# An attention and MLP kernel's generated order, built anew with another rule for the lock between VectorE and GpSimd

## The chip, the cores and the metric

The kernel runs on one core of one Trainium2 chip. The metric is the device time of one execution in microseconds, given as a median of three runs. Smaller is better. A profile is one further execution, read instruction by instruction. Engines are named as the profile names them: PE (TensorE matmuls), PEld (its weight loads), DVE (VectorE), ACT (ScalarE), POOL (GpSimd) and SP (SyncE, which issues the DMAs; SPq is its queue).

## What is computed

```python
# q, k, v: (4, 12, 448, 64) float32; w_in (768, 2048); w_out (2048, 768)
scores = scale * np.matmul(q, k.transpose(0, 1, 3, 2))
scores = np.where(mask, -1000000000.0, scores)          # causal
scores = scores - np.max(scores, axis=-1, keepdims=True)
attn = np.exp(scores)
attn = attn / (np.sum(attn, axis=-1, keepdims=True) + 1e-09)
x = np.matmul(attn, v)                                  # then (1792, 768)
h = x @ w_in
g = np.where(h >= 1, h, np.where(h <= -1, 0.0, (h + 1) ** 2 / 4))
return g @ w_out
```

## The kernel before

**Stages.** There are 24 pairs of heads (4 batches of 6). For a pair the kernel loads q and k into `st` tiles, transposes them on DVE (L713), multiplies scores on PE (L835 for the first five pairs, L845 and L865 for the others), masks and takes the row maximum on DVE (L884), takes the exponential on ACT (L888), adds a small number to the row sum `su` (L894 on POOL or L896 on DVE), inverts it (L899, DVE), scales the row tile `e` (L769 POOL, L771 ACT or L772 DVE), transposes it on PE (L785), copies it out of PSUM into `pt` (L816 ACT or L821 DVE) and multiplies with v on PE (L913). The result `x` feeds the first MLP product (L608): 16 blocks of 128 columns of w_in for each batch, 18 matmuls a block, and behind each block ACT `r` (L618), DVE `vv` (L621) and a product `r` on DVE (L627) or, as two instructions, on POOL (L624 and L625). There is a single `vv` buffer. `r` is stored to DRAM (`g_scratch`).

The second MLP stage loads `z` from `g_scratch`, forms sums and products of blocks of seven (a scheme with seven products in place of eight), and multiplies on PE (L1028) in seven token pairs. The first of these token pairs also needs w_out's 56 blocks, read back from DRAM as `w2`, `wn`, `st`, `sr`, `w` and `w3` tiles.

**Split into two parts.** Every matmul operand outside the first five pairs' scores is split in a rounded part (a copy: L462 ACT, L463 DVE, L464 POOL) and a residual (a subtraction: L471 DVE, L472 POOL). So each of q (`tt`), k (`ks`), `x`, w_in (`w<-wn`), w_out (`w<-w` and its like) and `hl` costs one copy and one subtraction. The line numbers L462 to L472 are those of the helpers that all of them share.

**What sets the order.** No loop issues these instructions. All of them are tasks of a planner (`Plan`), each with one or more alternatives: an engine, a cost, a function. `run` plays the tasks against a clock of its own, picks at each step the task that can start first and the engine for it, and emits it. Each engine then runs its instructions strictly in that order. `solve` does this some 100 times, disturbing the due times between the plays by the fixed random numbers in `STEPS` (`shake`), and the last play is the program. An alternative is marked as holding a lock (the planner calls it `port`) that DVE and POOL share; `PEN` is a penalty in microseconds on leaving the first alternative for one on another engine.

The planner's PSUM tiles matter below: the first MLP stage's last blocks and the second stage's products take turns on the same `s` banks, four of them, so a product waits until `vv` (L621) has read the block that was there.

Of the kernel before, what the change touches and what calls it, by code (L numbers as in the profile page):

```python
# [15 lines left out]
ALU = mybir.AluOpType  # L16
# [17 lines left out]
class Task:  # L34
    def __init__(self, alts, prio):
# [5 lines left out]
        self.lat = 1.6  # L41

# [5 lines left out]
class Plan:  # L48
# [98 lines left out]
    def solve(self):  # L147
# [4 lines left out]
        for ahead in (22.0,):  # L152
            for pen in (0.4,):
                self.AHEAD, self.PEN = ahead, {"DVE": pen, "ACT": 0.1}
# [29 lines left out]
    )  # L184

    def shake(self, seed):

        rng = random.Random(seed)
# [6 lines left out]
        kind = rng.randrange(3)  # L195
# [15 lines left out]
    def run(self, dry=False):  # L211
# [9 lines left out]
        while left:  # L221
# [21 lines left out]
            for prio, _, s, t in can:  # L243
                e0, c0, _, p0 = t.alts[0]
                c0 = 0.0 if e0 == "PE" else c0
                own = max(s, free.get(e0, 0.0) + queued.get(e0, 0.0), port if p0 else 0.0) + c0
                for a, (e, c, _, p) in enumerate(t.alts):
# [3 lines left out]
                    if a and st + c + queued.get(e, 0.0) + self.PEN.get(e, 0.0) >= own:  # L251
                        continue
                    chosen.setdefault(e, []).append(((st, prio), t, a, st, 0.0 if e == "PE" else c))
                queued[e0] = queued.get(e0, 0.0) + c0
            for e, cands in chosen.items():
                first = min(cands, key=lambda x: x[0])
                limit = first[3] + self.LOOK * first[4]
                key, t, a, st, _ = min((x for x in cands if x[3] <= limit and x[0][1] <= first[0][1]),
                                       key=lambda x: (x[0][1], x[0][0]))
                if best is None or key < best[0]:  # L260
                    best = (key, t, a, st)
# [845 lines left out]
```

## Time and profile before

| what | value |
|---|---|
| device time, median of 3 runs | 633.13 us (631.77 to 633.73) |
| the profiled execution's own time | 630.88 us |
| its span, first to last instruction | 629.1 us |
| busy PE, DVE, ACT, POOL | 607.3, 467.3, 340.9, 208.5 us |
| granted TensorE clock | 1.00 up to 600 us, 0.98 behind it |

The profiled execution is 2.25 us below the median of the three timed runs and 0.89 us below the fastest of them. A busy PE includes the time in which a matmul is still in its pipeline, so two matmuls that follow each other overlap in that sum. "Idle" and "wait" rows count only the time in which an engine had nothing in it.

The attention and the first MLP stage fill the span to about 417 us; the second MLP stage follows, with two blocks of the first one among its first products.

### The profile page before, as it was taken

To read this page: it belongs to the slowest core of one execution; us is meant where nothing else is said; L and a number is where in the kernel's file an instruction comes from. 1 tells how busy PE (TensorE), PEld (TensorE's weight loads), DVE (VectorE), ACT (ScalarE), POOL (GpSimd) and SP (SyncE) were. 2 spreads that over 40 slices of the span, in tenths; PEclk is the share of its full clock that TensorE was granted. 3 is DMA by queue.
4 is the path that set the end of the run, shared out by engine and by line. 5 is a ranking of instruction groups with operands and counts; after the bars stand their busy time and mean duration, and the time that the engine had idled before them with its cause. 6 is when DMAs were issued, how large, how long until landed. Compare 5 with 4: busy or idle time off the path is not lost.

```text
span 629.1 us, 11519 instructions
## 1 busy us (share of the span) xinstructions
PE 607.3 (97%) x3652; PEld 527.1 (84%) x3652; DVE 467.3 (74%) x1197; ACT 340.9 (54%) x851; POOL 208.5 (33%) x353
## 2 busy tenths in 40 slices
PE   7889999999999999999999999989999999999997
PEld 4455678797789798778798778979999999999997
DVE  4788898979996868976766619998766675665763
ACT  3888896748894546993554826845232322222320
POOL 3657765725661304681142606321101010110110
PEclk9999999999999999999999999999999999999999
DMA  8888789558868877668854119955423233424321
GB/s 212 235 198 214 188 244 278 143 165 244 252 192 272 245 241 228 167 204 244 260 160 162 31 51 324 329 177 191 118 84 118 72 118 83 131 68 118 105 83 64
DMA packets 96589, 110.33 MB, mean 175 GB/s; under 512 B 33552, under 2 KB 86288, under 8 KB 96528
## 3 DMA queue, kind: packets, MB, share of 16 engines
q1 hardware_dynamic: 96336, 109.15, 58.7%
q8 instruction: 29, 0.48, 0.3%
q10 hardware_dynamic: 192, 0.44, 0.2%
q14 instruction: 32, 0.26, 0.1%
HBM read 78.36 MB, written 31.20 MB: 174 GB/s over the span
## 4 chain that ended last, share of the span: by engine, by line
PE 73%; DMA 10%; DVE 7%; ACT 5%; issue 2%; POOL 1%; SPq 1%; ACTq 0%; DVEq 0%; POOLq 0%
PE h L608 21%; PE s L1028 16%; PE h L1028 8%; PE t L1028 8%; PE t L913 6%; DMA w<-in_moe_w_in_dram 6%; PE s L608 5%; PE t L785 5%; PE s L865 3%; ACT e L888 2%; DMA sr<-in_moe_w_out_dram 2%; DMA st<-in_q_dram 1%; DVE vv L621 1%; PE s L845 1%; DVE w L471 1%
## 5 line engine op out<-in xcount | busy, mean ns | idle before, releaser
L608 PE MATMUL h<-x,w 128*128 128x448 f32 x900 | 204.0, 372 | 2.7 <-DVE vv L621 2.2
L608 PEld LDWEIGHTS h<-x,w 128*128 128x128 f32 x900 | 162.3, 188 | 16.4 <-DVE vv L621 4.0
L462 ACT ACTIVATE hl<-z 128x896 fp32r<-128x896 f32 x56 | 53.5, 955 | 135.4 <-DVE z L471 93.9
L1028 PE MATMUL s<-w,hl 128*128 128x384 f32 x534 | 101.6, 335 | 3.1 <-DVE vv L621 3.1
L1028 PEld LDWEIGHTS s<-w,hl 128*128 128x128 f32 x534 | 93.5, 188 | 3.5 <-DVE vv L621 3.4
L888 ACT ACTIVATE e<-s,mn 128x128 f32<-128x128 f32 (+6 forms) x168 | 81.4, 496 | 16.0 <-DVE mn L884 11.8
L471 DVE TENSOR_TENSOR z<-z 128x128 f32<-128x128 f32 x196 | 54.4, 312 | 43.4 <-DMA z<-g_scratch 41.2
L884 DVE CUSTOM_DVE_ANT_0 s<-s,mask 128x128 f32<-128x128 f32 (+5 forms) x168 | 72.5, 468 | 8.9 <-PE s L835 4.9
L471 DVE TENSOR_TENSOR hl<-z,hl 128x896 fp32r<-128x896 f32 x54 | 60.4, 1126 | 15.8 <-ACT hl L462 15.7
L785 PE MATMUL t<-ident,e 128*128 128x128 f32 (+1 forms) x384 | 61.8, 279 | 5.6 <-ACT pt L818 1.8
L472 POOL TENSOR_TENSOR z<-z 128x128 f32<-128x128 f32 x28 | 12.6, 467 | 154.2 <-DMA z<-g_scratch 121.4
L785 PEld LDWEIGHTS t<-ident,e 128*128 128x128 f32 (+1 forms) x384 | 43.4, 139 | 20.5 <-ACT pt L816 3.0
L769 POOL TENSOR_SCALAR e<-e,su 128x256 f32<-128x256 f32 (+5 forms) x95 | 52.3, 556 | 24.0 <-DVE su L899 17.4
L618 ACT ACTIVATE r<-h,half 128x448 f32<-128x448 f32 x50 | 31.5, 635 | 45.9 <-PE h L608 44.4
L713 DVE STREAM_TRANSPOSE qs<-st 128x448 f32<-128x448 f32 x48 | 46.3, 968 | 11.2 <-DMA st<-in_q_dram 7.4
L816 ACT ACTIVATE pt<-t 128x256 f32<-128x256 f32 (+2 forms) x117 | 49.3, 445 | 8.3 <-PE t L785 7.9
L1028 PE MATMUL h<-w,hl 128*128 128x384 f32 x258 | 52.8, 335 | 0.0
L1028 PE MATMUL t<-w,hl 128*128 128x384 f32 x258 | 52.7, 335 | 0.0
L608 PE MATMUL s<-x,w 128*128 128x448 f32 x252 | 52.2, 364 | 0.4 <-DVE vv L621 0.4
L621 DVE TENSOR_TENSOR vv<-h,r 128x448 f32<-128x448 f32 x50 | 31.0, 620 | 26.7 <-ACT r L618 26.5
L913 PE MATMUL t<-pt,vr 128*64 128x448 f32 (+3 forms) x384 | 50.3, 391 | 0.5 <-ACT pt L816 0.4
L608 PEld LDWEIGHTS s<-x,w 128*128 128x128 f32 x252 | 46.9, 188 | 3.8 <-DVE vv L621 0.7
(103 smaller groups left out, 881.2 us busy)
## 6 DMA issues: line engine op xcount, KB each, us to landing
g_scratch<-r SPq DMA_DIRECT2D x64, 224.0 KB, 3.1
z<-g_scratch SPq DMA_DIRECT2D x56, 256.0 KB, 2.9
sr<-in_moe_w_out_dram SPq DMA_DIRECT2D x32, 384.0 KB, 4.4
w<-in_moe_w_in_dram SPq DMA_DIRECT2D x28, 384.0 KB, 4.8
w_scratch<-wn SPq DMA_DIRECT2D x56, 192.0 KB, 3.5
st<-in_q_dram SPq DMA_DIRECT2D x94, 108.0 KB, 3.4
st<-in_k_dram SPq DMA_DIRECT2D x94, 108.0 KB, 3.6
w<-w_scratch SPq DMA_DIRECT2D x50, 192.0 KB, 4.2
```

Of the source, the lines that this page charges most:

```text
L462: "ACT": ("ACT", act(n, 0.04), lambda: nc.scalar.activation(out=dst(), in_=src(), func=ACTF.Copy)),
L471: "DVE": ("DVE", dve(n), lambda: nc.vector.tensor_tensor(out=dst(), in0=x(), in1=y(), op=op), port),
L608: nc.tensor.matmul(out=h[:, :S], lhsT=wi[f][kk // K2][:, a, kk % K2 * P:(kk % K2 + 1) * P], rhs=x[:, c], start=(kk == 0 and n == 0), stop= ...
L621: task([("DVE", dve(S), lambda: nc.vector.tensor_tensor(out=y.tile, in0=h[:, :S], in1=r.tile, op=ALU.max))], g0, reads=[(h, 0), (r, 0)], w ...
L713: task([("DVE", 0.81, lambda g=g, t=t: nc.vector.transpose(out=x[g].tile.rearrange("p (r c) -> p c r", c=C), in_=bands(t[:, :32])))], prio ...
L769: ("POOL", pool_ts(n, 0.09), lambda: nc.gpsimd.tensor_scalar(out=ev(), in0=ev(), scalar1=sc(), scalar2=1.0, op0=ALU.mult, op1=ALU.mult), T ...
L785: nc.tensor.transpose(t[:k, c:c + P], es[i][:, j * P:j * P + k], ident)
L816: nc.scalar.activation(out=dst(), in_=src(), func=ACTF.Copy)
L884: task([("DVE", dve(n) + (0.05 if n < 384 else 0.02), lambda s=s, off=off, n=n, i=i: nc.vector.tensor_tensor_reduce(out=s[:, off:off + n], ...
L888: task([("ACT", act(n, 0.19), lambda s=s, off=off, n=n, i=i: nc.scalar.activation(out=es[i][:, :n], in_=s[:, off:off + n], func=ACTF.Exp, ...
L913: nc.tensor.matmul(out=o[64 * g:64 * g + 64, j * P:S], lhsT=vr[:k, j, g, :], rhs=pt[:k, 7 * j:5 * j + NI, g, :] if j < NJ - 1 else pt[:k, ...
L1028: nc.tensor.matmul(out=acc[x][:, :NO], lhsT=hl[:, a, i * P:(i + 1) * P], rhs=(hi, lo)[c](), start=(f == 0 and n == 0), stop=(f == KF - 2 a ...
```

## The change

Four edits, all in the planner:

- When `run` compares the engines' candidates, it took the one that could start first. It now takes the one that asks first, which is the time at which its data and its engine are there, whether or not the lock is free. So the lock goes to the first to ask.
- `PEN` on going to DVE falls from 0.4 to 0.1 us, and going to POOL, which had none, costs 12 us. An alternative on POOL that is a task's first one isn't touched by it.
- A task may start its list of alternatives at another place (`first`), which `shake` sets at random in a fourth kind of disturbance.
- One DVE alternative (the small addition to `su`) is marked as holding the lock.

`STEPS` is another list of numbers.

```diff
         self.nom = self.moved = None
         self.lat = 1.6
+        self.first = 0
...
-            for pen in (0.4,):
-                self.AHEAD, self.PEN = ahead, {"DVE": pen, "ACT": 0.1}
+            for pen in (0.1,):
+                self.AHEAD, self.PEN = ahead, {"DVE": pen, "ACT": 0.1, "POOL": 12.0}
...
     STEPS = (
-        1000008, 1000015, 1000095, 1000120, 1000197, 1000199, 1000222, 1000307, 1000343, 1000359, 1000388,
...
+        4000005, 4000025, 4000028, 4000035, 4000046, 4000085, 4000091, 4000095, 4000118, 4000121, 4000146,
...
-        kind = rng.randrange(3)
+        kind = rng.randrange(4)
+        if kind == 3:
+            for t in self.tasks:
+                if a <= t.begin <= z and t.moved is None and len(t.alts) > 1 and rng.random() < part:
+                    t.first = rng.randrange(len(t.alts))
+            return
...
-                e0, c0, _, p0 = t.alts[0]
+                e0, c0, _, p0 = t.alts[t.first]
...
-                for a, (e, c, _, p) in enumerate(t.alts):
+                for n in range(len(t.alts)):
+                    a = (t.first + n) % len(t.alts)
+                    e, c, _, p = t.alts[a]
...
-                    if a and st + c + queued.get(e, 0.0) + self.PEN.get(e, 0.0) >= own:
+                    if n and st + c + queued.get(e, 0.0) + self.PEN.get(e, 0.0) >= own:
                         continue
-                    chosen.setdefault(e, []).append(((st, prio), t, a, st, 0.0 if e == "PE" else c))
+                    chosen.setdefault(e, []).append(((st, prio), t, a, st, 0.0 if e == "PE" else c,
+                                                     st if e == "PE" else max(s, free.get(e, 0.0))))
...
+                key = asked, t.prio if t.nom is None else t.nom
                 if best is None or key < best[0]:
...
-                out=su[:, a:z], in0=su[:, a:z], scalar1=1e-9, scalar2=None, op0=ALU.add))],
+                out=su[:, a:z], in0=su[:, a:z], scalar1=1e-9, scalar2=None, op0=ALU.add), True)],
```

What this does to the program is seen in the order of each engine's instructions. DVE has 66 more, POOL 54 fewer, ACT 2 fewer, and PE issues the same matmuls in a somewhat different order. By kind:

| step | DVE | ACT | POOL |
|---|---|---|---|
| residual of `tt` | 4 to 14 | | 15 to 5 |
| other subtractions of 384 columns and those of `ks` | 77 to 96 | | 62 to 43 |
| copies (rounded parts of `ks`, `tt`, `qb`, `w`, `x`) | 5 to 26 | 112 to 124 | 65 to 32 |
| scaling of `e` | 1 to 14 | 72 to 75 | 95 to 79 |
| copies out of PSUM to `pt` (L816, L821) | 22 to 39 | 117 to 100 | |
| product `r` (two instructions on POOL) | 63 to 53 | | 1 to 11 |

In the three places below, a number behind a name tells buffers apart; "waits" lists the engines or DMA queues that the instruction waits for. After the change the lines from L275 on stand 12 further down (L471 is L483).

**DVE at the change of stage.** Before, the residuals of seven `w` blocks stand ahead of the last-but-one `vv`, the one that frees the bank of the third product of the second stage:

```order
L621 TENSOR_TENSOR vv_5375<-s_5288,r_5365 128x448 [waits DVE_49,Activation_49]
L627 SCALAR_TENSOR_TENSOR r_5365<-r_5365,vv_5375 128x448 [waits DMAHW5_49,DVE_49]
L471 TENSOR_TENSOR hl_5333<-z_5085,hl_5333 128x896
L471 TENSOR_TENSOR w_5238<-w_5238 128x384 [waits DMAHW6_49]
L471 TENSOR_TENSOR w_5260<-w_5260 128x384 [waits DMAHW1_49,PE_49]
L471 TENSOR_TENSOR w_5285<-w_5285 128x384 [waits DMAHW4_49,PE_49]
L471 TENSOR_TENSOR w_5277<-w_5277 128x384 [waits DMAHW3_49]
L471 TENSOR_TENSOR w_5367<-w_5367 128x384 [waits DMAHW2_49,PE_49,Activation_49]
L471 TENSOR_TENSOR w_5386<-w_5386 128x384 [waits DMAHW4_49,Activation_49]
L471 TENSOR_TENSOR w_5345<-w_5345 128x384 [waits DMAHW0_49]
L621 TENSOR_TENSOR vv_5433<-s_5350,r_5418 128x448 [waits DVE_49,Activation_49]
```

With the change:

```order
L633 TENSOR_TENSOR vv_5378<-s_5299,r_5367 128x448 [waits DVE_49,Activation_49,Pool_49]
L483 TENSOR_TENSOR w_5063<-w_5063 128x384
L639 SCALAR_TENSOR_TENSOR r_5367<-r_5367,vv_5378 128x448 [waits DMAHW5_49,DVE_49]
L483 TENSOR_TENSOR w_5055<-w_5055 128x384
L483 TENSOR_TENSOR z_5271<-z_5271 128x128
L483 TENSOR_TENSOR w_5069<-w_5069 128x384 [waits DMAHW7_49]
L483 TENSOR_TENSOR z_5271<-z_5271 128x128 [waits Pool_49]
L483 TENSOR_TENSOR w_5117<-w_5117 128x384
L483 TENSOR_TENSOR z_5316<-z_5316 128x128 [waits DMAHW7_49]
L483 TENSOR_TENSOR w_5155<-w_5155 128x384
L633 TENSOR_TENSOR vv_5424<-s_5343,r_5412 128x448 [waits DVE_49,Activation_49]
```

From the first `vv` of the last 16 to the fifteenth, which is the last row of both pieces, DVE had 75 instructions and now has 61: 21 residuals of `w` blocks are 6, 14 products `r` are 11 (three went to POOL), and four residuals of `w2`, `wn`, `st` and `sr` blocks came in.

**POOL at the same place.** Before, residuals only; with the change a copy that waits for a DMA, and behind it one of the three products `r`:

```order
L472 TENSOR_TENSOR w_5170<-w_5170 128x384 [waits DMAHW5_49,PE_49,Activation_49]
L472 TENSOR_TENSOR w_5251<-w_5251 128x384 [waits DMAHW0_49,PE_49,Activation_49]
L472 TENSOR_TENSOR w_5215<-w_5215 128x384 [waits DMAHW3_49]
L472 TENSOR_TENSOR w_5268<-w_5268 128x384 [waits DMAHW2_49,PE_49,Activation_49]
L472 TENSOR_TENSOR w_5348<-w_5348 128x384 [waits DMAHW1_49,PE_49,Activation_49]
L472 TENSOR_TENSOR z_5399<-z_5399 128x128 [waits DMAHW6_49,DVE_49,Pool_49]
```

```order
L484 TENSOR_TENSOR w_5135<-w_5135 128x384 [waits DMAHW0_49]
L484 TENSOR_TENSOR w_5162<-w_5162 128x384 [waits DMAHW3_49]
L476 TENSOR_SCALAR w_5280<-w_5280 128x384 [waits DMAHW3_49,PE_49]
L636 TENSOR_SCALAR r_5337<-r_5337 128x448 [waits DMAHW5_49,DMAHW6_49,DMAHW1_49,DVE_49]
L637 TENSOR_TENSOR r_5337<-r_5337,vv_5348 128x448 [waits Pool_49]
L484 TENSOR_TENSOR z_5271<-z_5271 128x128 [waits DMAHW2_49,DVE_49]
```

The `vv_5378` and the second `z_5271` in DVE's piece wait for these last rows.

**POOL and DVE at the first pair with split operands.** Before, POOL made q's copy, its residual and `qb` in a row, between two scalings:

```order
L464 TENSOR_SCALAR tt_681<-qs_658 128x448 [waits DVE_49]
L769 TENSOR_SCALAR e2_137<-e2_137,su_572 128x192 [waits DVE_49]
L769 TENSOR_SCALAR e0_134<-e0_134,su_572 128x64 [waits PE_49]
L472 TENSOR_TENSOR tt_681<-qs_658,tt_681 128x448 [waits Pool_49]
L464 TENSOR_SCALAR qb1_145<-tt_681 64x2x64 [waits Pool_49]
L472 TENSOR_TENSOR w_685<-wn_532,w_685 128x384 [waits Activation_49]
```

With the change ACT makes the copy and DVE the residual, between copies of `pt` and an inverse:

```order
L833 COPY pt_669<-t_722 128x3x128 [waits PE_49]
L483 TENSOR_TENSOR tt_702<-qs_688,tt_702 128x448 [waits Activation_49]
L833 COPY pt_669<-t_741 128x256 [waits PE_49]
L911 RECIPROCAL su_711<-su_711 128x2 [waits Pool_49]
L475 CAST qb1_145<-tt_702 64x2x64 [waits DVE_49]
```

## Rows read from the trace of the kernel before

**Rows 1.** The page: the span, and busy time of each engine with its instructions.

```profile
span 629.1 us, 11519 instructions
...
PE 607.3 (97%) x3652; PEld 527.1 (84%) x3652; DVE 467.3 (74%) x1197; ACT 340.9 (54%) x851; POOL 208.5 (33%) x353
```

**Rows 2.** Windows of 50 us: length, then busy us (instructions), clock, DMA share, GB/s.

```profile
core 0: us, PE busy (x) PEld busy (x) DVE busy (x) ACT busy (x) POOL busy (x), PEclk, DMA share, GB/s
...
50.00:100.00 50.00, 46.50 (x304) 35.55 (x305) 43.95 (x127) 42.32 (x126) 32.88 (x54) 1.00 0.82 223
100.00:150.00 50.00, 48.99 (x292) 41.37 (x291) 43.49 (x103) 32.71 (x81) 26.70 (x37) 1.00 0.67 199
150.00:200.00 50.00, 49.35 (x327) 40.52 (x326) 44.65 (x134) 38.43 (x118) 24.16 (x46) 1.00 0.79 234
...
500.00:550.00 50.00, 50.00 (x290) 49.98 (x289) 32.69 (x73) 13.71 (x16) 3.53 (x8) 1.00 0.36 104
```

**Rows 3.** Windows of 10 us around the change of stage, same columns.

```profile
400.00:410.00 10.00, 10.00 (x52) 9.37 (x51) 9.90 (x19) 7.14 (x15) 3.97 (x4) 1.00 0.94 319
410.00:420.00 10.00, 9.14 (x47) 8.32 (x45) 9.69 (x18) 5.64 (x11) 2.41 (x3) 1.00 0.52 156
420.00:430.00 10.00, 7.78 (x45) 7.78 (x46) 7.82 (x17) 2.97 (x4) 0.98 (x2) 1.00 0.52 170
430.00:440.00 10.00, 10.00 (x59) 10.00 (x58) 9.11 (x19) 6.08 (x11) 2.49 (x2) 1.00 0.72 232
```

**Rows 4.** PE's longest waits, whole span: total us, times, longest.

```profile
PE s L1028 <- DVE vv L621: 3.1, 1, 3.1
```

**Rows 5.** The order of time, DVE and PE at that wait: start, us, [idle before <-releaser].

```profile
416.44 1.91 DVE L471 TENSOR_TENSOR hl<-z,hl 128x896 fp32r<-128x896 f32 x1
...
418.28 3.36 DVE L471 TENSOR_TENSOR w<-w 128x384 fp32r<-128x384 f32 x7
...
421.56 0.61 DVE L621 TENSOR_TENSOR vv<-s,r 128x448 f32<-128x448 f32 x1
...
422.22 0.79 PE L1028 MATMUL s<-w,hl 128*128 128x384 f32 x3 [3.08 <-DVE vv L621]
```

**Rows 6.** PE's waits from 16 to 110 us, the three longest of eleven that sum to 9.9.

```profile
PE h L608 <- DVE vv L621: 1.9, 3, 0.7
PE t L785 <- ACT pt L818: 1.8, 1, 1.8
PE s L835 <- ACT e L888: 1.6, 2, 1.5
```

**Rows 7.** The order of time: a DVE instruction that begins under one of POOL.

```profile
385.24 2.13 POOL L472 TENSOR_TENSOR hl<-z,hl 128x896 fp32r<-128x896 f32 x1
385.46 0.62 DVE L621 TENSOR_TENSOR vv<-s,r 128x448 f32<-128x448 f32 x1 [0.56 <-ACT r L618]
386.12 1.74 DVE L627 SCALAR_TENSOR_TENSOR r<-r,vv 128x448 f32<-128x448 f32 x1
```

**Rows 8.** Groups by line: count, busy us, mean ns, idle time before.

```profile
L769 POOL TENSOR_SCALAR e<-e,su 128x256 f32<-128x256 f32 (+5 forms) x95 | 52.3, 556 | 24.0 <-DVE su L899 17.4 <-PE t L785 1.9 <-DVE su L896 1.5
L627 DVE SCALAR_TENSOR_TENSOR r<-r,vv 128x448 f32<-128x448 f32 x63 | 45.6, 723 | 1.2
L472 POOL TENSOR_TENSOR tt<-qs,tt 128x448 fp32r<-128x448 f32 x15 | 17.6, 1171 | 0.6 <-ACT tt L462 0.2
L821 DVE COPY pt<-t 128x384 f32<-128x384 f32 (+1 forms) x22 | 11.0, 509 | 1.5 <-PE t L785 1.4
L471 DVE TENSOR_TENSOR tt<-qs,tt 128x448 fp32r<-128x448 f32 x4 | 2.5, 626 | 0.0
L463 DVE CAST x<-t 128x448 fp32r<-128x448 f32 x4 | 2.5, 620 | 0.0
L624 POOL TENSOR_SCALAR r<-r 128x448 f32<-128x448 f32 x1 | 1.7, 1723 | 0.0
L625 POOL TENSOR_TENSOR r<-r,vv 128x448 f32<-128x448 f32 x1 | 1.2, 1156 | 0.1
L772 DVE TENSOR_SCALAR e<-e,su 128x256 f32<-128x256 f32 x1 | 0.5, 507 | 0.0
L463 DVE CAST w<-wn 128x384 fp32r<-128x384 f32 x1 | 0.4, 360 | 0.0
```

**Rows 9.** POOL's waits for a block of w_out: total us, times, longest.

```profile
POOL w L464 <- DMA w<-w_scratch: 7.5, 2, 5.4
```

More of the change, by code (lines that the diff above doesn't have):

```diff
@@ L257, in run @@
                 limit = first[3] + self.LOOK * first[4]
-                key, t, a, st, _ = min((x for x in cands if x[3] <= limit and x[0][1] <= first[0][1]),
+                _, t, a, st, _, asked = min((x for x in cands if x[3] <= limit and x[0][1] <= first[0][1]),
                                        key=lambda x: (x[0][1], x[0][0]))
+                key = asked, t.prio if t.nom is None else t.nom
                 if best is None or key < best[0]:
```

20 rows, old and new, of the table STEPS are left out of this document.

## The prediction, made before the changed kernel ran

> **What bounds the kernel now.** I read the busy times first. PE is busy for 607.3 of 629.1 us, DVE for 467.3, POOL for 208.5 [rows 1]. So PE has some 22 us with nothing in it, and no edit that leaves its matmuls alone can win more than a few of them. Then the windows. From 500 to 550 us PE and its loads are both full and 290 matmuls pass in 50 us, with DVE at 32.7 [rows 2]: the second MLP stage is PE's, and an order can't shorten it. From 50 to 200 us PE is busy for 46.5, 49.0 and 49.4 of each 50, and DVE for 44.0, 43.5 and 44.7 [rows 2]: here DVE is nearly as full as PE. Thirdly the change of stage: DVE is busy for 9.90 and 9.69 of the two stretches of 10 us from 400 to 420 us, and PE falls to 7.78 in the next one [rows 3]. Last the waits. PE's longest is 3.1 us, once, for one `vv` [rows 4]. The order of time shows why: a residual of 1.91 us and seven residuals of w blocks in 3.36 us stand ahead of that `vv` on DVE, and PE's next product starts 3.08 us late, right behind it [rows 5]. In the attention stage PE's visible waits from 16 to 110 us sum to 9.9 us, in eleven kinds of which the longest have 1.9, 1.8 and 1.6 us [rows 6]; there is no single one to remove.
>
> **The change part by part.** *Same matmuls.* PE issues the same ones in nearly the same order, so its own work costs nothing more or less. What can move is what it waits for.
>
> *The change of stage.* DVE's 75 instructions up to the fifteenth `vv` become 61. Eleven fewer are residuals (15 of `w` out, 4 of other blocks in), at 3.36 / 7 = 0.48 us each [rows 5]: 5.3 us. Three fewer are products `r` at 0.72 us [rows 8]: 2.2 us. That `vv` can thus come up to 7.5 us earlier on DVE, while PE waited 3.08 us for it; the wait would be gone with 4.4 us to spare. But the eleven residuals aren't saved. They come later, in a stretch where DVE has 2.2 and 0.9 us idle of each 10 [rows 3], and the three `r` take POOL 1.72 + 1.16 = 2.88 us each [rows 8], with the lock. So the gain lies between nothing (the backlog shows up a few products later) and 3.1 us. I take 2.3, three quarters of it: the row says the deadline was missed for order and not for want of time, since DVE's idle time in the next 20 us, 3.1 us, is already as long as the wait.
>
> *Work from POOL to DVE in the attention stage.* At durations of [rows 8]: 10 residuals of `tt` at 0.63 us are 6.3 us for DVE, where POOL took 1.17 each; 19 other subtractions at the same price 11.9; 13 scalings at 0.51 are 6.6; 17 copies to `pt` at 0.51 are 8.7; 21 copies between 0.36 and 0.62 are 7.6 to 13.0; ten products `r` fewer, at 0.72, are -7.2. Together 34 to 39 us, some 1.5 us a pair over 24 pairs. The cover is DVE's idle time: 150 - 132.1 = 17.9 us from 50 to 200 us [rows 2], and more behind that. POOL loses 10 x 1.17 of `tt`, 16 x 0.56 = 8.9 of scalings, and the rest of the subtractions and copies, and gets 10 x 2.88 = 28.8 us of `r` back [rows 8]. Where a chain runs over these steps it gets shorter: 0.63 for 1.17 us for a residual, 0.51 for 0.56 for a scaling.
>
> *The lock.* A product `r` that begins at 386.12 us under a POOL subtraction of 2.13 us takes 1.74 us, where the `vv` ahead of it, of the same size, takes 0.62: it ends 0.49 us behind POOL's end at 387.37 [rows 7]. So the later one stands until the other is through. The mean of all 63 is 0.72 [rows 8], some 0.1 us above that. The Trainium skill says the same (SBUF — State Buffer, section "SBUF: two separate sides"): the shared pair of ports is an exclusive lock, held for the whole instruction by whichever starts first. By that rule, and the trace agrees, a planner that gives the lock to the first to ask plans the waits where they happen, while dividing the bandwidth would have made the first edit worthless. What fewer POOL instructions save of such waits is small: 54 instructions less of 358 are a seventh, while `r` puts long ones back.
>
> Of PE's 9.9 us of waits in the attention stage [rows 6] I take a tenth, 1.0 us, as won by shorter chains and a truer plan of the lock. The row that bounds it from above is that sum: half of it, 5 us, is the most I would believe. From below the bound is DVE's fullness: with 1.5 us more a pair over the nine or so pairs from 50 to 200 us, 14 us, DVE has some 4 us left of its 17.9.
>
> *The tail and the second stage* keep their order and cost: zero, with PE's full windows as cover.
>
> The sum against the profiled execution: 629.1 - 2.3 - 1.0 = 625.8 us of span, with the 1.8 us around it 627.6 of its own time (630.88 before). I carry the difference of 3.3 us to the median, which lies 2.25 us above that execution: 633.13 - 3.3 = 629.8 us.
>
> **The rivals.**
>
> *DVE becomes the bound (slower).* Place: the pairs from 50 to 200 us. DVE there would go from 132.1 to some 146 of 150 us busy. An engine that works strictly in order at 97% can't catch up after a late copy or maximum, and PE has few other matmuls until the first MLP stage has material. If 6 of the 14 us come through to PE, and the 2.3 us at the change of stage are won, the time is 633.1 + 6 - 2.3 = 636.8. It turns into a loss that can be measured from 4.2 us on. For it: DVE at 44 of 50 already. Against it: the planner takes DVE only where it would finish sooner than the first choice, so much of the work goes into idle time; and behind 110 us the first MLP stage gives PE matmuls for a late pair. The Trainium skill speaks for this rival (Perfetto Trace Analysis, section "Optimizing Scalar/DVE Operations"): work is to be taken off DVE where DVE is saturated, to ScalarE or even GpSimd, though between GpSimd and DVE it may not help because of the shared port. The change does the opposite in the stretch in which DVE is fullest; no row here shows yet which half of that sentence holds.
>
> *POOL's product holds the change of stage.* At POOL's place shown above, a copy waits for a block's DMA, the product `r` of 2.88 us stands behind it, then a sum of `z` for which DVE waits ahead of the fifteenth `vv`. POOL has waited for such a block for up to 5.4 us [rows 9]. 5.4 + 2.9 us less the 3.6 us or so that PE takes for a block of 18 matmuls at some 0.2 us (52 and 51 matmul records of both stages in 10 us [rows 3]) leaves 4.7, so the wait of 3.1 would become up to 4.7: with the 1.0 us of the attention stage 633.7, no change.
>
> *The wait only moves.* DVE's whole load between 400 and 450 us stays as it is; the late residuals make a product wait a few rows further on. Then only the 1.0 us remain: 632.1. The change of the planner's rule would have done nothing that the chip can show.
>
> *More is won.* Half of the 9.9 us and 2.3 us: 633.1 - 7.3 = 625.8.
>
> **How the numbers follow.** About 0.3%, 1.9 us, is what a measurement can tell from no change here. The forecast, 627.5 to 632 with 629.8 likeliest, gets 0.50, a tenth of which lies within 0.3%. More won: 0.10. DVE the bound: 0.18, of which 0.02 within 0.3%. POOL's product: 0.08, of which 0.06 within. The wait only moves: 0.14, within. Faster: 0.45 + 0.10 = 0.55. Same: 0.05 + 0.02 + 0.06 + 0.14 = 0.27, slower: 0.16 + 0.02 = 0.18. The range goes from 624.8, a little below the case of more, to 636.8, the middle of the slower rival; about half of that rival and a little at the lower end stay out. Faster and slower cases together hold most of the chance, so the likeliest one's own range is repeated: 627.5 to 632.
>
> **What would show it.** Right: no wait of PE for `vv` over 1 us at the first products of the second stage; PE's busy time from 410 to 430 us near 19 of 20; DVE's sum near 500 us and POOL's below 200; the first product of the second stage some 1 us earlier than before (417 us), and the rest of the gain right behind it. Wrong: PE's waits from 16 to 110 us above 12 us, with DVE at 47 or more of 50 from 50 to 200 (the first rival); a wait of DVE for POOL's `r` or `z` ahead of the fifteenth `vv` (the second); a new wait of PE for a `w` block or `hl` between 420 and 445 us (the third). The prediction falls as a whole if the time from 0 to 110 us moves by more than 5 us either way, since it treats that stretch as nearly unchanged.

## The result, and the profile after

The changed kernel takes **627.33 us** in the median (626.3 to 627.71, 4 runs), the kernel before 632.45 us beside it (630.62 to 633.73, 4 runs): ratio 0.9919, 95% interval 0.9889 to 0.9948, which is 3.3 to 7.0 us less. Forecast were 629.8 us and a range of 624.8 to 636.8: the time lies in the range, 0.2 us below the part of it that was called likeliest (627.5 to 632). The profiled execution took 627.59 us (630.88 before): the 3.3 us of the sum. That this fits to the digit is luck, since executions of one and the same order lie several us apart (623.29 to 629.39 us in e2 below). Its page has the span of the sum, 625.8 us:

```profile
span 625.8 us, 11517 instructions
...
PE 606.7 (97%) x3652; PEld 524.9 (84%) x3652; DVE 475.0 (76%) x1263; ACT 338.0 (54%) x849; POOL 193.0 (31%) x299
```

POOL fell by 15.5 us, as the order had told, but DVE rose by 7.7 us only [rows 1]. The same 50-us windows as in [rows 2] (columns: length, busy us and instructions of each engine, clock, DMA share, GB/s):

```profile
50.00:100.00 50.00, 49.18 (x318) 39.70 (x315) 45.18 (x131) 43.19 (x124) 26.25 (x45) 1.00 0.80 217
100.00:150.00 50.00, 49.34 (x320) 38.79 (x319) 47.26 (x132) 36.92 (x101) 26.70 (x37) 1.00 0.64 180
150.00:200.00 50.00, 49.43 (x297) 41.26 (x295) 39.60 (x100) 27.59 (x74) 15.43 (x23) 1.00 0.86 245
...
500.00:550.00 50.00, 50.00 (x290) 50.00 (x289) 31.95 (x73) 13.16 (x15) 8.43 (x10) 1.00 0.36 105
```

From 50 to 100 us PE does 2.7 us more than before; from 280 to 400 us it does 4.4 us less (windows in the section on that stretch). The second stage is as full as it was. The change of stage answers to [rows 3]:

```profile
410.00:420.00 10.00, 10.00 (x54) 9.54 (x53) 7.16 (x18) 5.28 (x10) 4.13 (x4) 1.00 0.61 200
420.00:430.00 10.00, 9.67 (x56) 9.35 (x55) 10.00 (x23) 3.58 (x6) 0.00 (x0) 1.00 0.59 174
430.00:440.00 10.00, 10.00 (x60) 10.00 (x59) 9.87 (x22) 6.18 (x11) 0.55 (x1) 1.00 0.52 171
```

PE is busy for 19.67 of the 20 us from 410 to 430, 16.92 before. Of the wait of 3.1 us for `vv` [rows 4] 0.3 us is left, and the waits from 16 to 110 us, 9.9 us before [rows 6], sum to 3.2 (PE's waits, 400 to 440 us, and then the three longest of the five from 16 to 110 us: total, times, longest):

```profile
PE s L1040 <- DVE vv L633: 0.3, 1, 0.3
```

```profile
PE t L797 <- ACT e L783: 1.4, 1, 1.4
PE t L797 <- DVE pt L833: 0.7, 1, 0.7
PE s L847 <- DVE qs L725: 0.5, 1, 0.5
```

So PE won time at two places and gave some back at a third. To add it up I use one measure for every kernel, **PE's excess**: for each matmul record the time to the next one's start, less what its columns need at 2.25 a ns (the second stage runs 290 products of 384 columns in 50 us [rows 2], 2.23 a ns), summed by the time at which it starts. It holds waits, short gaps and the slower clock of the first microseconds. A transpose of 128 columns takes longer than this count gives it, some 0.11 us from start to start, and two products on half of the rows each run side by side and take less. Every kernel has as many of both, so the measure compares kernels and is not PE's idle time. Executions of one order differ in it by some 3 us in the first 80 us and by up to some 2 us in each later stretch.

```
PE's excess, us           0-80  80-280  280-400  400-440   median us   ratio to before
before                    26.9    17.4      7.1      3.8      632.45
changed                   20.5    17.6     12.5      1.0      627.33   0.9919
e1  early part alone      20.8    26.3      7.8      6.1      637.23   1.0083
e2  change of stage alone 24.8    19.1      7.3      0.4      627.02   0.9917
e3  three parts           22.0    17.4     29.7      0.3      646.17   1.0228
e4  one vv moved          25.8    19.5      6.9      5.7      631.88   0.9988
e5  changed, old end      23.7    17.2     11.0      8.7      636.33   1.0070
e6  both vv moved         26.1    17.7      7.5      2.9      629.19   0.9974
e7  eight r on DVE        22.6    17.2      8.1      0.5      623.93   0.9876
e8  3.4 us more at 62 us  19.1    18.3     10.2      0.7      629.86   0.9970
e9  old engines, 0-80     22.0    17.0     10.7      0.8      627.13   0.9897
e10 all r on DVE          20.9    17.7      8.7      0.5      623.05   0.9819
e11 before, no search     28.5    20.4      9.5      5.3      639.58   1.0115
e12 changed, no search    27.1    18.2      7.7      2.0      630.65   0.9971
```

(In e8 the added matmuls count as work by their columns, 5.5 us, where they take 3.4; without them its first number would be 21.1.) Between the two profiles: -6.4, +0.2, +5.4 and -2.8 us. The expectations below name 24.5 us for the kernel before from 0 to 80 us, and 50.1 and 49.4 us for the sums from 0 to 400 us of the kernel before and the changed one. By one count for all kernels, that of the table, these are 26.9, 51.4 and 50.6 us.

### The profile page after: what moved, and what is told of

It is laid out like the page before. It is cut to its first block, busy times and chain, and to the rows that moved or that the text cites. A ratio compares the mean times of both kernels' runs of the same rounds, so it can differ in the third digit from the quotient of the medians.

```text
span 625.8 us, 11517 instructions
## 1 busy us (share of the span) xinstructions
PE 606.7 (97%) x3652; PEld 524.9 (84%) x3652; DVE 475.0 (76%) x1263; ACT 338.0 (54%) x849; POOL 193.0 (31%) x299
## 4 chain that ended last, share of the span: by engine, by line
PE 54%; DVE 16%; DMA 11%; ACT 8%; issue 4%; POOL 3%; SPq 3%; DVEq 0%; ACTq 0%; POOLq 0%
PE s L1040 16%; PE h L620 12%; PE h L1040 8%; PE t L1040 8%; PE t L925 4%; DMA st<-in_k_dram 4%; DVE s L896 3%; ACT e L900 3%; PE t L797 3%; SPq L466 3%; DVE vv L633 3%; DMA w<-in_moe_w_in_dram 2%; DVE qs L725 2%; DMA w<-w_scratch 2%; DVE r L639 2%
## 5 line engine op out<-in xcount | busy, mean ns | idle before, releaser
L620 PE MATMUL h<-x,w 128*128 128x448 f32 x900 | 206.2, 373 | 3.2 <-DVE vv L633 2.9
L474 ACT ACTIVATE hl<-z 128x896 fp32r<-128x896 f32 x53 | 50.5, 953 | 119.0 <-DVE z L483 86.8
L483 DVE TENSOR_TENSOR hl<-z,hl 128x896 fp32r<-128x896 f32 x51 | 56.4, 1106 | 43.5 <-ACT hl L474 43.3
L900 ACT ACTIVATE e<-s,mn 128x256 f32<-128x256 f32 (+6 forms) x168 | 81.2, 490 | 14.8 <-DVE mn L896 9.4
L896 DVE CUSTOM_DVE_ANT_0 s<-s,mask 128x256 f32<-128x256 f32 (+6 forms) x168 | 72.8, 465 | 7.2 <-ACT e L900 3.1
L483 DVE TENSOR_TENSOR z<-z 128x128 f32<-128x128 f32 x202 | 54.3, 302 | 8.7 <-DMA z<-g_scratch 6.3
L781 POOL TENSOR_SCALAR e<-e,su 128x128 f32<-128x128 f32 (+5 forms) x79 | 44.2, 563 | 41.9 <-DVE su L911 28.6
L630 ACT ACTIVATE r<-h,half 128x448 f32<-128x448 f32 x50 | 31.3, 631 | 41.0 <-PE h L620 36.5
L484 POOL TENSOR_TENSOR z<-z 128x128 f32<-128x128 f32 x22 | 10.7, 488 | 133.2 <-DVE z L483 59.4
L925 PE MATMUL t<-pt,vr 128*64 128x448 f32 (+3 forms) x384 | 50.1, 391 | 0.0
L828 ACT ACTIVATE pt<-t 128x384 f32<-128x384 f32 (+2 forms) x100 | 42.9, 448 | 8.2 <-PE t L797 7.8
```

The lines of the kernel that those rows point to most:

```text
L474: "ACT": ("ACT", act(n, 0.04), lambda: nc.scalar.activation(out=dst(), in_=src(), func=ACTF.Copy)),
L483: "DVE": ("DVE", dve(n), lambda: nc.vector.tensor_tensor(out=dst(), in0=x(), in1=y(), op=op), port),
L620: nc.tensor.matmul(out=h[:, :S], lhsT=wi[f][kk // K2][:, a, kk % K2 * P:(kk % K2 + 1) * P], rhs=x[:, c], start=(kk == 0 and n == 0), stop= ...
L781: ("POOL", pool_ts(n, 0.09), lambda: nc.gpsimd.tensor_scalar(out=ev(), in0=ev(), scalar1=sc(), scalar2=1.0, op0=ALU.mult, op1=ALU.mult), T ...
L828: nc.scalar.activation(out=dst(), in_=src(), func=ACTF.Copy)
L896: task([("DVE", dve(n) + (0.05 if n < 384 else 0.02), lambda s=s, off=off, n=n, i=i: nc.vector.tensor_tensor_reduce(out=s[:, off:off + n], ...
```

## The experiments

All but the last two replay a recorded order: the planner is left out and the table of its result stands in its place, so that one thing can be changed and all else keeps its place.

```diff
-        plan.solve()
+        plan.replay()
```

### The stages one by one (e1, e2, e3, e5)

The four runs put the order of one kernel in front of the order of the other.

> The tasks are emitted in a recorded order and on recorded engines instead of a planned one: the order of the changed kernel for the 610 tasks that it plans before 80 us, and behind them the other 3018 in the order of the kernel before. Theory (the gains stand at places that add up): PE's time above its own matmul work from 0 to 80 us falls from 24.5 to about 20.5 us as in the changed kernel, the rest stays as in the kernel before (the wait of 3.1 us for vv at the change of stage too), span 629.1 - 4.0 = 625.1 us. Rival (a lead isn't kept: DVE or the pairs' chains set the end of the attention stage anyway): the excess from 80 to 400 us grows by 3 to 4 us and the span is 628 to 629.

> Recorded order again: the order and engines of the kernel before for the 2662 tasks that it plans before 395 us, behind them the remaining 966 in the order of the changed kernel. Theory: only the change of stage gets better, the wait of 3.1 us for vv goes, and PE's excess from 400 to 440 us falls from 3.8 to about 1 us; span 629.1 - 2.5 = 626.6 us (626.0 to 627.0). Rival (the wait only moves, since DVE has too much work from 400 to 450 us): some other wait of 2 to 3 us up to 450 us, span 628.5 to 629.5.

> Recorded order in three parts: the changed kernel's for the 2013 tasks that it plans before 285 us, the order before for the 649 that this plans before 395 us, the changed kernel's for the remaining 966. Theory (the changed kernel gives back about 5 us from 280 to 400 us by its order there, products r on POOL among it): that stretch has PE's excess of the kernel before, about 7 instead of 12.5 us, and the span is 625.8 - 5 = 621 us, faster than both. Rival (the excess there is the price of the lead: with less time lost earlier, matmuls that could fill the gaps of the last pairs are gone): excess 11 to 13 us from 280 to 400 us as in the changed kernel, span 625 to 627.

> The complement of the run on the change of stage alone: recorded order and engines of the changed kernel for the 2665 tasks that it plans before 395 us, behind them the other 963 in the order of the kernel before. Theory (the change of stage carries the whole gain and the attention stage next to none, as PE's excess summed over 0 to 400 us says: 50.1 us before, 49.4 in the changed kernel): the wait of about 3 us for vv is there again and the time is that of the kernel before, span 628 to 630, ratio 0.997 to 1.003. Rival (attention and change of stage each give a part): span 626 to 627.5, ratio near 0.995.

**e2** gave 627.02 us, ratio 0.9917 (0.9886 to 0.9948), span 625.7: the order of the change of stage alone brings all that the whole change brings. Its excess from 400 to 440 us is 0.4 us, 3.4 less than before.

**e1** (ratio 1.0083, 1.0050 to 1.0115) and **e3** (1.0228, 1.0196 to 1.0259) answer nothing. Both became slower by what happens at the seam: in e1 the excess from 80 to 100 us is 11.2 us (2.5 before), in e3 one wait of 20.2 us begins at 297 us (PE's waits from 280 to 320 us in e3: total, times, longest).

```profile
PE h L620 <- DVE vv L633: 21.1, 3, 20.2
```

There the two orders disagree on how far the decoding of w_out should be, the overdue blocks come all at once, and DVE waits for them in order ahead of a `vv`: 15.3 us in five waits for `wn`. Neither kernel has such a place, so whether an early lead lasts had to be asked in another way (e8).

**e5**, the complement of e2, is slower than both: 636.33 us, ratio 1.0070 (1.0040 to 1.0099), and both of its expectations were too low. PE waits 4.8 us for a `vv` and 0.8 for another. The order of time shows what was slow ahead of it (start, us; DVE first, then POOL):

```profile
405.83 1.90 DVE L483 TENSOR_TENSOR hl<-z,hl 128x896 fp32r<-128x896 f32 x1
407.65 1.38 DVE L483 TENSOR_TENSOR sr<-sr 128x384 fp32r<-128x384 f32 x1
408.95 1.36 DVE L483 TENSOR_TENSOR w<-w 128x384 fp32r<-128x384 f32 x1
410.24 1.10 DVE L483 TENSOR_TENSOR z<-z 128x128 f32<-128x128 f32 x1
411.26 1.37 DVE L483 TENSOR_TENSOR w<-w 128x384 fp32r<-128x384 f32 x1
412.56 2.08 DVE L483 TENSOR_TENSOR z<-z 128x128 f32<-128x128 f32 x2
...
416.76 0.61 DVE L633 TENSOR_TENSOR vv<-s,r 128x448 f32<-128x448 f32 x1
```

```profile
406.74 1.86 POOL L484 TENSOR_TENSOR st<-st 128x384 fp32r<-128x384 f32 x1
408.58 1.32 POOL L484 TENSOR_TENSOR w<-w 128x384 fp32r<-128x384 f32 x1
409.86 1.33 POOL L484 TENSOR_TENSOR sr<-sr 128x384 fp32r<-128x384 f32 x1
411.14 4.34 POOL L484 TENSOR_TENSOR w<-w 128x384 fp32r<-128x384 f32 x4
```

The two engines take turns: from `sr` to the first `z` each DVE instruction ends 0.15 to 0.43 us behind one of POOL (409.03 behind 408.60, 410.31 behind 409.90, 411.34 behind 411.19). In the changed kernel a `z` takes 0.28 us, a w residual 0.55 and an `hl` 1.08 (rows below). The seven instructions from `hl` to the last two `z` take 9.2 us, summed, and would take 1.08 + 3 x 0.55 + 3 x 0.28 = 3.6. That is the lock of [rows 7] at every instruction, as the Trainium skill has it (SBUF — State Buffer, section "SBUF: two separate sides": the loser blocks fully). Since e5 has a seam too, as e1 and e3 have, it shows what the lock can do to a row, and not what the parts of the change are worth.

### The change of stage (e4, e6)

Both are the order of before with `vv` and `r` moved up among the seven w residuals on DVE. What DVE does there in a row, before, in e4 and in e6 (in e6 three w residuals stand between the two pairs, not two):

```diff
-hl w w w w w w w vv r z vv z w z r
+hl w w vv r w w w w w z vv z w z r
```

```diff
-hl w w w w w w w vv r z vv z w z r
+hl w w vv r w w w vv r w w z z w z
```

> The recorded order of the kernel before with one move: the vv for which PE waits 3.1 us and the r behind it stand behind the second of the seven w residuals on DVE and no longer behind the seventh (with them, on ACT, the relu that they need stands ahead of one w copy). Theory (a deadline missed for order): PE's wait falls from 3.1 to about 1 us, since the relu ends at 419.3 us and vv can then end at 420; span 629.1 - 2.1 = 627.0. Rival (DVE has no time to give, the wait only moves): PE waits 2 to 3 us for a w residual or hl a few products later, span 628.5 to 629.5.

> The recorded order of the kernel before. On DVE the last two vv of the first stage, each with the r behind it, stand ahead of w residuals that were ahead of them: the first behind two of the seven, the second behind the next two of them (the last of PE's first-stage products stands one place earlier for it, and a relu on ACT). With the first alone moved PE waited twice for vv, 1.9 and 1.4 us. Theory (a deadline missed for order, and it is two deadlines): PE's waits for vv from 416 to 430 us sum to at most 1.2 us instead of 3.1, nothing comes behind, ratio about 0.996 to 0.997. Rival (DVE's amount of work up to there decides): 2.5 us or more of waits remain, for vv or for a w residual, ratio 0.998 to 1.001.

With one `vv` moved nothing is won (ratio 0.9988, 0.9965 to 1.0012): the wait is cut in two, and the second one stands before the next `vv`, which is now late (PE, order of time in e4):

```profile
421.15 0.79 PE L1040 MATMUL s<-w,hl 128*128 128x384 f32 x3 [1.36 <-DVE vv L633]
...
424.90 0.78 PE L1040 MATMUL s<-w,hl 128*128 128x384 f32 x3 [1.91 <-DVE vv L633]
```

With both moved 1.8 us of waits for `vv` and 0.5 for an `hl` remain, and the time is 629.19 us, ratio 0.9974 (0.9946 to 1.0002): some 1.6 us, an interval that just takes in no change, between the theory and the rival. That two deadlines were missed for order fits e4 and e6, but it isn't shown clear of noise; the excess from 400 to 440 us falls by 0.9 us here and by 3.4 in e2. Two more things differ. The first is to be seen on DVE in the changed kernel:

```profile
416.00 0.55 DVE L483 TENSOR_TENSOR w<-w 128x384 fp32r<-128x384 f32 x1
416.47 0.28 DVE L483 TENSOR_TENSOR z<-z 128x128 f32<-128x128 f32 x1
416.67 0.55 DVE L483 TENSOR_TENSOR w<-w 128x384 fp32r<-128x384 f32 x1
417.14 0.61 DVE L633 TENSOR_TENSOR vv<-s,r 128x448 f32<-128x448 f32 x1
...
422.96 1.08 DVE L483 TENSOR_TENSOR hl<-z,hl 128x896 fp32r<-128x896 f32 x1
```

Every one has its short time. In the kernel before, the `hl` ahead of the seven residuals took 1.91 us [rows 5], and these two `z` just before:

```profile
409.11 2.12 DVE L471 TENSOR_TENSOR z<-z 128x128 f32<-128x128 f32 x2
```

Those are 0.83 and 1.56 us above 1.08 and 0.56, together 2.4 us of lock in the row up to the `vv` for which PE waited 3.1.

The second is the amount of work. From the first `vv` of the last 16 to the fifteenth (windows of before, of e6, of the changed kernel; the third number is DVE's busy time):

```profile
376.17:422.17 46.00, 42.62 (x213) 39.36 (x211) 44.68 (x75) 31.05 (x61) 17.77 (x16) 1.00 0.83 275
```

```profile
375.89:419.89 44.00, 42.63 (x213) 39.36 (x211) 42.51 (x70) 30.75 (x60) 17.49 (x16) 1.00 0.81 273
```

```profile
374.02:417.75 43.73, 42.40 (x212) 39.12 (x211) 33.94 (x62) 29.18 (x56) 25.42 (x22) 1.00 0.93 311
```

DVE is nearly full in the kernel before and in e6. In the changed kernel it is busy for 33.9 of 43.7 us, in e2 for 36.5 of 42.3, because more residuals stand behind the two deadlines. Whether that smaller load or the missing lock makes the rest of e2's gain stays open: no run took either away alone.

### What the stretch from 280 to 400 us gives back (e7, e10)

PE is idle for 5.3 of these 120 us in the changed kernel and for 0.9 before (windows of before, of the changed kernel, of e7):

```profile
280.00:340.00 60.00, 59.63 (x342) 51.41 (x342) 40.59 (x92) 27.54 (x69) 15.50 (x25) 1.00 0.72 223
340.00:400.00 60.00, 59.43 (x360) 50.30 (x357) 39.27 (x102) 39.20 (x103) 24.64 (x37) 1.00 0.46 148
```

```profile
280.00:340.00 60.00, 56.94 (x329) 47.74 (x328) 37.91 (x98) 25.48 (x61) 19.70 (x17) 1.00 0.69 220
340.00:400.00 60.00, 57.75 (x338) 48.45 (x338) 44.88 (x121) 38.03 (x99) 25.03 (x34) 1.00 0.65 209
```

```profile
280.00:340.00 60.00, 59.17 (x344) 50.76 (x343) 43.70 (x114) 26.77 (x65) 5.08 (x8) 1.00 0.72 228
340.00:400.00 60.00, 58.86 (x347) 49.92 (x346) 47.34 (x118) 39.08 (x98) 21.47 (x30) 1.00 0.68 224
```

DVE isn't full there. Its own waits name the cause, DVE's longest from 280 to 400 us:

```profile
DVE vv L633 <- POOL r L637: 12.9, 5, 3.1
```

One of them in order of time (POOL, DVE, PE):

```profile
327.40 2.11 POOL L636 TENSOR_SCALAR r<-r 128x448 f32<-128x448 f32 x1 [0.25 <-DVE vv L633]
329.60 1.16 POOL L637 TENSOR_TENSOR r<-r,vv 128x448 f32<-128x448 f32 x1
330.79 0.62 DVE L633 TENSOR_TENSOR vv<-h,r 128x448 f32<-128x448 f32 x1 [2.84 <-POOL r L637]
331.47 2.88 PE L620 MATMUL h<-x,w 128*128 128x448 f32 x13 [0.78 <-DVE vv L633]
```

`vv` has a single buffer, and `r` reads it. While POOL is at `r`, the next `vv` stands at the head of DVE's queue, all of DVE stands behind it, and PE waits for the bank of `h` that this `vv` would free. In e7 the only edit is the engine of eight `r`:

```diff
-r, planned at 290 to 400 us: POOL (L636, L637)
+r, planned at 290 to 400 us: DVE (L639)
```

> The recorded order of the changed kernel with 8 products r that it plans for POOL between 285 and 400 us done by DVE at the same place (0.7 us there instead of two instructions and 2.9 us on POOL). Theory (POOL's long r, and the lock that it holds, cost what the changed kernel gives back from 280 to 400 us): PE's excess there falls from 12.5 to about 8 us and the span from 625.8 to 622 to 623. Rival (the stretch is late for other reasons): excess 12 to 13.5 us and the span within 1 us of 625.8.

> The recorded order of the changed kernel with all its 11 products r of POOL done by DVE at the same place, three more (planned at 119, 137 and 179 us) than in the run that moved eight. Theory (each r on POOL costs its own share of time, 3.4 us for eight): another 0.5 to 1.3 us less, span 621 to 621.8, median 622.6 to 623.4. Rival (POOL's r hurts only where PE has no other work to put in, behind 280 us; from 110 to 180 us the first MLP stage fills the gaps): same time as with eight, 623.5 to 624.5, PE's excess from 80 to 280 us as before, 17 us.

e7: 623.93 us (623.2 to 625.4; the changed kernel 626.3 to 627.7), ratio 0.9876 (0.9842 to 0.9910), span 622.2, excess from 280 to 400 us 8.1 us (10.2 to 12.5 in the four executions that have the changed kernel's order there, `r` on POOL). The theory's numbers hold; the runs lie apart from those of the changed kernel, though the intervals of the two ratios still overlap. The edit takes away the wait for the buffer together with the lock that POOL's `r` holds; the 12.9 us are the wait. **e10** with all eleven is at 623.05 us, ratio 0.9819 (0.9780 to 0.9858), span 621.4. It is the fastest of all, measurably faster than the changed kernel (whose interval begins at 0.9889). Its median lies in the theory's range, but from e7 it can't be told apart, and PE's excess from 80 to 280 us, 17.7 against 17.2, shows no gain where the three early ones stood, as the rival has it.

Why did a planner that charges 12 us for POOL as a second choice still take it? It plans `r` there as 0.53 + 1.09 = 1.62 us. The trace has nearly twice that (groups by line: count, busy us, mean ns, idle before):

```profile
L636 POOL TENSOR_SCALAR r<-r 128x448 f32<-128x448 f32 x11 | 20.2, 1834 | 38.8 <-DVE vv L633 38.2 <-POOL qb L476 0.4 <-DMA w<-w_scratch 0.2
L637 POOL TENSOR_TENSOR r<-r,vv 128x448 f32<-128x448 f32 x11 | 12.7, 1154 | 0.9
...
L781 POOL TENSOR_SCALAR e<-e,su 128x448 f32<-128x448 f32 x11 | 7.9, 718 | 6.4 <-DVE su L911 5.5 <-PE t L797 0.5 <-DVE qb L475 0.3
```

And the search draws the first choice of engine at random (the new field `first`), so an `r` on POOL as first choice pays no penalty. That this is how the eleven came there is argued from the code, not shown; it fits that the plan without the search (e12) has all 64 `r` on DVE.

### Does an early lead last, and what brings it (e8, e9)

```diff
-                for m, a0, n in todo:
+                for m, a0, n in todo * (5 if n_pair == 6 and len(todo) == 2 else 1):
```

> The recorded order of the changed kernel; in the pair whose first wide scores stand at 61.1 us on PE, that block of matmuls, 1.02 us, is issued five times instead of once (it starts each sum anew, so the scores are the same): 4.1 us more for PE at one place of the attention stage. Theory (PE is the bound and an early lead or lag lasts): the span grows by 3.5 to 4.1 us, ratio to the changed kernel 1.006. Rival (a lead isn't kept, because up to the change of stage the time is set by DVE and the chains of the pairs): the lag shrinks on the way, PE's excess from 80 to 400 us falls by 3 us or more and the span grows by 1 us at most.

> The recorded order of the changed kernel; of the tasks that it plans before 80 us, the 51 that another engine does in the kernel before are given back to that engine at the same place: POOL gets 24 and loses 12 (copies of tt, ks, qs and qb, scalings, residuals, small sums of su). Theory (work taken off POOL is what shortens the chains of the first pairs): PE's excess from 0 to 80 us, 20.5 to 23.7 us in five runs with the changed kernel's order there and 24.5 to 26.1 in four with the order before, goes up by 3 us or more to 25 to 28, and the time by about as much, ratio to the kernel before 0.996 to 1.000. Rival (the new order on DVE and PE does it, whatever the engines): excess stays at 21 to 24, ratio 0.990 to 0.993.

In e8 the block takes 4.53 us instead of 1.09, 3.4 us more and not 4.1 (e8, then the changed kernel):

```profile
62.05 4.53 PE L877 MATMUL s<-ks,tt 64*128 64x384 f32 x60
```

```profile
61.10 1.09 PE L877 MATMUL s<-ks,tt 64*128 64x384 f32 x12
```

The span grew by 2.2 us, the median by 2.5 (629.86, ratio 0.9970, 0.9944 to 0.9997): between theory and rival. Up to the block e8 is 1.0 us behind. A later score of a pair stands at 270.02 us against 264.66 in the changed kernel, 5.4 us late, and one at 317.53 against 314.48, 3.1 us late. Two more executions of the same order, e5 and e9, have the first at 267.70 and 265.50 us, the second at 316.95 and 315.04. So a lag of 2.3 to 5.4 us is left at 270 us and one of 0.6 to 3.1 at 318. That a lag lasts so far and shrinks behind 270 us, in the stretch where the changed kernel waits for POOL's `r` anyway, fits this but isn't clear of the scatter.

e9 gave 51 early tasks back to their old engines (POOL gets 27, not 24). The time stayed: 627.13 us, ratio 0.9897 (0.9857 to 0.9937), excess from 0 to 80 us 22.0. So the rival holds: not the moves off POOL but the new order makes the early gain, some 4 us (25.9 on the mean of the four runs with the order of before, 21.8 on that of the six others with the new one, e8 and e9 left out).

### The rule without the search (e11, e12)

```diff
-    STEPS = (
...
+    STEPS = ()
```

> The kernel before with an empty table of steps: its planner's first plan, without the recorded search. Theory (the search gives an order its length, the rule of the lock little): slower than the kernel before by 5 to 12 us, and within 3 us of the changed kernel without its search. Rival (the rule and the penalties carry the gain): slower than the changed kernel without its search by 4 us or more.

> The changed kernel with an empty table of steps: the lock granted to the first to ask and the new penalties alone. Theory (the search gives the length): slower than the changed kernel by 5 to 12 us, within 3 us of the kernel before without its search. Rival (rule and penalties carry the gain): at or below the kernel before with its search, 632 us, and 4 us or more below the kernel before without it.

Without search the kernel before takes 639.58 us (1.0115, 1.0088 to 1.0142), the changed one 630.65 (0.9971, 0.9946 to 0.9996): 8.9 us apart. The theory falls and the rival holds in these two plans: rule and penalties carry the gain, and an unsearched plan under the new rule is no slower than the searched one under the old. What they do is plain on the page (e11, then e12):

```profile
PE 611.7 (96%) x3652; PEld 529.0 (83%) x3652; DVE 468.1 (73%) x1212; ACT 341.4 (53%) x854; POOL 197.4 (31%) x334
```

```profile
PE 606.5 (96%) x3652; PEld 525.7 (84%) x3652; DVE 487.6 (78%) x1294; ACT 343.0 (55%) x855; POOL 128.8 (20%) x251
```

POOL is busy 68.6 us less, DVE 19.5 us more, and the time falls. The search then wins 7.7 us for the kernel before (631.88 beside these runs) and 3.3 for the changed one, and brings POOL back to 193.0 us, `r` among it. Rule and penalties were not run apart, and each plan is one sample of what its planner makes.

## Why the prediction was right, and where not

**The change of stage: right, and too small.** Taken were 2.3 us of at most 3.1. The two profiles give 2.8, e2 gives 3.4 in the excess and 3.3 to 7.2 us by its ratio, both above 3.1. The place is shown (e2), the reason only in part. A deadline missed for order fits, but there were two deadlines (e4), order alone gave 1.6 us that are not clear of noise (e6), and the prediction had left out that some 2.4 us of DVE's row ahead of that `vv` were the lock. Against its words "for order and not for want of time" stands that DVE was busy for 44.7 of the 46.0 us of that row. The signs named for it came: no wait over 1 us for `vv`, PE busy for 19.67 of 20 us, the first product of the second stage at 415.9 us instead of 417.3. POOL's sum came below 200 us (193.0), DVE's not near 500 (475.0).

**The attention stage: the number right, the working wrong.** One tenth of 9.9 us was taken, 1.0 us; up to 400 us the excess fell by 0.8. That is the sum of parts that the prediction did not see: 6.4 us won before 80 us (some 4 on the means, e9), nothing from there to 280, 5.4 lost from 280 to 400. That they nearly cancel to the 1.0 us is luck. Its own test, that 0 to 110 us moves by no more than 5 us, failed in the two profiles: the scores that stood at 100.10 us come at 92.47 us, with as many matmuls ahead of them:

```profile
100.10 0.77 PE L845 MATMUL s<-ks,qb 128*128 128x448 f32 x3
```

```profile
92.47 0.78 PE L857 MATMUL s<-ks,qb 128*128 128x448 f32 x3
```

In e2, e4 and e6, with the order of before, they stand at 97.9 to 98.9 us, in e5, e7, e9 and e10, with the new one, at 94.2 to 96.0: on the means, the two profiles included, that is 4.5 us and just within the 5.

The step that failed is the bound "half of it, 5 us, is the most" together with the silence on 280 to 400 us: only waits that existed before were priced there, and the new one came from work that the change brings. The waits from 16 to 110 us fell by 6.7 us, more than that bound.

**DVE's load: mis-sized by a factor of four to five.** 34 to 39 us were to come on DVE; 7.7 came, and from 50 to 200 us nothing (132.0 us, 132.1 before). `tt` came as priced, 6.3 us, `pt` with 7.4 us for 8.7. But "19 other subtractions" at 0.63 us were 11.9 us in the sum, and the groups for `ks`, `wn`, `w` and `hl` give 1.3 + 2.2 + 5.4 - 4.0 = 4.9 us, since larger ones went the other way. And instructions got shorter where POOL left the lock: `r` went from 0.72 to 0.68 us each, 9.4 us less for ten fewer, and the 28 `wn<-w,wn` from 17.8 to 15.1 us. A part is the count itself: the profile's DVE records overlap by some 0.07 us each, so their durations, summed, grew by 17.5 us (547.9 to 565.5) where the busy time grew by 7.7. (Two readings were off without weight: POOL had 353 instructions before, not 358 [rows 1], and of the 52 and 51 records in 10 us the 51 are PEld's; PE has 59 in the second stage [rows 3].)

**The lock: called small, and too quickly.** The prediction read the rule from [rows 7] rightly and priced it by the mean of `r`, 0.1 us each. e5 shows 5.6 us of it on one row of seven instructions, and before the change 2.4 us of it stood ahead of the deadline that was missed; a mean over the span hides such rows. e11 and e12 price the rule together with its penalties at 8.9 us, on one plan each and with 68.6 us less work on POOL. What the lock alone is worth no run shows.

**The rivals.** *DVE the bound* did not come: DVE took work and got no fuller where it was full. Its sentence from the Trainium skill (Perfetto Trace Analysis, section "Optimizing Scalar/DVE Operations") has two halves, and only the second, that moving work between GpSimd and DVE might not help, is borne out here: `r` on POOL cost time, and taking it back won some (e7, e10). That was at a place where DVE was busy for 82.8 of 120 us; the first half, on a saturated DVE, no run here tests by itself. *POOL's product* was the right mechanism, and its sign came at its own place: ahead of the fifteenth `vv` DVE waited three times for POOL's `r`, 7.7 us in all, the last time here (changed kernel):

```profile
413.11 0.62 DVE L633 TENSOR_TENSOR vv<-s,r 128x448 f32<-128x448 f32 x1 [2.84 <-POOL r L637]
```

PE lost next to nothing by that last one, since DVE had less to do in that row and PE was busy without a gap from 410 to 420 us. From 280 to 400 us, where the other two of these waits lie and which the rival for the most part did not name, the same mechanism cost 12.9 us of DVE's time and some 3.4 us of the kernel's. *The wait only moves* is what e4 did, with half of the edit. *More is won*, 625.8 us, is nearer to 627.33 than the forecast's 629.8 is, 1.5 against 2.5 us.

## What to carry to other kernels

Where two engines share a lock, look for instructions that take a multiple of their shortest time right ahead of a deadline, and count how much work stands ahead of it; a mean over the span hides both. An engine that is slow at a step costs more than its time if the step holds the only buffer that the next instruction of a faster, in-order engine needs: price the queue behind it. And a planner searches its own costs: check the durations of what it newly uses (1.62 us planned, 2.99 measured) before trusting what it picked.

## What was not expected of the hardware

On POOL a product of 128 x 448 with a minimum in it (L636) takes 1.83 us, a scaling of the same size (L781) 0.72: the pair of operations matters, not only the size. And the granted clock of the first 20 us differs between executions of one and the same order: from 10 to 20 us its mean over the two levels, 1.2 and 2.4 GHz, is 0.87 in the changed kernel, 0.80 in e5 and 0.94 in e7, which place the same instructions there; PE had been busy for 6.66, 6.66 and 5.85 of the 10 us ahead. PE's excess of the first 80 us is 20.5, 23.7 and 22.6 us, so the clock alone doesn't explain its spread.
